# Row numbers of an indirect gather written by iota on GpSimd, and the gather moved to the head of GpSimd's list

## The chip, the cores and the metric

The kernel runs on one core of a Trainium2 chip. The metric is the device time of one execution in microseconds (us). A core has five engines that run their own instruction lists: TensorE (PE in the profile; PEld is its weight load), VectorE (DVE), ScalarE (ACT), GpSimd (POOL) and SyncE (SP). SP issues transfers only; POOL and ACT issue some as well. The transfers run on 16 DMA engines that all queues share: q1 in the profile carries what SP issues, q0 what POOL issues.

## The reference, cut to what matters

Two independent halves are computed and written side by side. The first is a linear attention with learned feature maps; the second, which this change touches, is a long convolution of `u` with a state-space kernel, done through a Fourier transform over 2L points.

```python
def _A_ref(x, wqkv, w_phi, wo):          # x: 1 x 2048 x 448, 16 heads of 28
    q, k, v = ...                        # x @ wqkv, split in heads
    phi_q = concat([softmax(q @ w_phi), softmax(-(q @ w_phi))])
    phi_k = concat([softmax(k @ w_phi), softmax(-(k @ w_phi))])
    o = (phi_q @ (phi_k^T @ v)) / (phi_q . sum_s phi_k + 1e-6)
    return o @ wo

def _B_ref(u, A_re, A_im, B_re, B_im, C_re, C_im, log_dt, Dskip):   # u: 1 x 2048 x 448, N = 256
    dt = exp(log_dt)
    P = exp(dt * (A_re + 1j A_im) * l)   # l = 0 .. 2047
    K = einsum("dn,dnl,dn->dl", C, P, dt * B).real
    y = irfft(rfft(pad(u)) * rfft(pad(K)))[:L]
    return y + u * Dskip

return concat([a, b], axis=-1)           # 1 x 2048 x 896
```

## The kernel before

The program is written as some 1,200 numbered units (an instruction or a few, with its tiles). A planner's result stands in the source as a written-out list, `ORDER`: each word is a unit's number and the engine that runs it (P, V, A, G, S for PE, DVE, ACT, POOL, SP). `Plan.run` records the units in that order, so each engine's list is the list of its own words, in their order. No scheduler moves them. Semaphore waits are put in where a unit reads or overwrites what another made. Transfers use eight semaphores per kind of queue in turn, so a transfer can also wait for the one eight places ahead of it.

The Fourier transform of `u` is done with the symmetry of the time axis: for each half `b` of 1,024 rows, `signal_spectrum` needs 512 rows in rising order and the 512 others mirrored. The first half of the tile `rw` comes by an ordinary load (unit 190 on SP, step `ua0.0`). The mirrored half comes by an indirect DMA (unit 191 on POOL, step `ua0.1`, line 610), which takes its 128 row numbers from the small tile `mirror` (128 x 2 int32, one column for each `b`). Each row is 3,584 bytes. `mirror` is filled by a load from a constant (unit 8 on POOL, step `rows`, line 446, issued in the helper `dma` at line 394).

Behind the gather, in the order in which they use each other:

- DVE, line 346: the difference and the sum of the two halves of `rw` (units 192 and 193, steps `ab0.0` and `ab0.1`).
- PE, line 379: the matmuls of the steps `us0.0` and `us0.1` (units 203, 196, 194, 201) with the cosine table `G1`, whose first half is loaded by unit 14 on SP. Their results are copied by ACT and DVE (line 369) and written to DRAM by transfers on SP and POOL (`SUd`).

Around it on POOL: unit 23 clears `zt`, which PE's idle matmuls at the start use (line 481); unit 17 clears the block-diagonal weight tile `BD` (line 464); units 19, 21 and 22 load pieces of `w_phi` into `BD`. The fourth piece, unit 20, stands in SP's list and waits for unit 17. Behind unit 20 in SP's list stand the loads of `G1` (14), of the attention weights (13), of `B_re` and `C_re` (5, 4), of a part of `x` (9), of the second half of `G1` (15), and then the first writes to `SUd`.

Of the kernel before, what the change touches and what calls it, by code (L numbers as in the profile page):

```python
# [50 lines left out]
def _round_bf16(a):  # L51
    import ml_dtypes
    return np.asarray(a, np.float32).astype(ml_dtypes.bfloat16)

def _row_positions():
    pos = np.full((N_KT, 128), -1)
    for kt, p0, h0, h1, runs in K_ROWS:
        r = p0
        for run in runs:
            for h in range(h0, h1):  # L60
                for lo in range(*run):
                    pos[kt, r] = HI[h] + LO[lo]
                    r += 1
    return pos

def _dft_tables():
    m = np.arange(512)
    w = np.pi * (4 * m + 1) / 2048.0
    phi = np.pi * np.outer(4 * m + 1, 4 * m + 1) / 4096.0
    GO = np.stack([np.cos(phi - np.pi / 4), np.cos(phi + np.pi / 4)])  # L70
    quad = np.arange(128)
    G = GO[:, np.stack([2 * quad, 2 * quad + 1, 510 - 2 * quad, 511 - 2 * quad])].transpose(2, 0, 1, 3)
    GO = GO.reshape(2, 4, 128, 512).transpose(2, 0, 1, 3)
    GI = np.stack([GO, GO[:, :, :, ::-1] * np.array([1.0, -1.0])[None, :, None, None]])
    e = _round_bf16(np.arange(2048)).astype(np.int64)
    pos = _row_positions()
    where = {int(p): (kt, r) for (kt, r), p in np.ndenumerate(pos)}
    assert set(e.tolist()) <= set(where)
    F = np.zeros((2, N_KT, 128, 4, 512))
    for blk in range(2):  # L80
        for l in range(1024):
            kt, r = where[int(e[1024 * blk + l])]
            even = np.exp(-1j * w * l) / 1024.0
            odd = np.exp(1j * (np.pi - w) * l) / 1024.0
            F[blk, kt, r] += np.stack([even.real, odd.real, even.imag, odd.imag])
    used = [(0, 0), (0, 1), (0, 2), (0, 3), (0, 4), (1, 4), (1, 5)]
    for blk in range(2):
        for kt in range(N_KT):
            assert (blk, kt) in used or not F[blk, kt].any()
    FT = np.stack([F[b, k] for b, k in used])  # L90
    FT = FT.reshape(7, 128, 16, 128).transpose(2, 1, 0, 3)
    pid = np.eye(128)[:, None, :] * np.array(DIAG).reshape(-1)[None, :, None]
    hm = np.zeros((112, 4, D_HEAD + 1))
    for hh in range(4):
        hm[hh::4, hh, :] = 1.0
    mirror = (256 * np.arange(2)[None, :] + 255 - np.arange(128)[:, None]).astype(np.int32)
    return (*(_round_bf16(t) for t in (G, GI, FT, pid, hm)), mirror)

ORDER = ("23G 42P 31P 43P 30P 33P 46P 0A 48A 49V 8G 32P 45P 38P 3S 1S 17G 2S 19G 6S 190S 50V 51V 53V 52V 56P 57V 54P 55A "
         "58P 59V 37P 84P 65A 63A 40P 64A 62A 85V 60P 82P 39P 61V 83V 191G 26P 25P 41P 47P 34P 27P 35P 44P 192V 193V 10S "  # L100
         "129P 20S 69A 70A 130V 66V 1098V 14S 125P 28P 29P 127P 126A 128V 13S 71V 203P 204A 196P 131P 194P 197A 201P 195V "
         "5S 132V 4S 202V 165P 153P 155P 166V 154V 156V 86P 78P 21G 88V 67A 72A 75A 73A 9S 89P 79A 80P 81A 15S 91V 167P "
         "151P 87V 90V 109A 108A 152V 117P 200S 198G 199G 118V 119P 168V 149P 120V 74V 22G 150A 207S 7S 12S 210P 211A 36P "
# [72 lines left out]
class Plan:  # L176
# [5 lines left out]
    def step(self, label, base, phase=None):  # L182

        self.now = label
        return phase
# [49 lines left out]
    def run(self):  # L235
        places, done = iter(PLACES), set()
        for word in ORDER.split():
            u, e = self.units[int(word[:-1])], ENGINES[word[-1]]
# [55 lines left out]
def kernel(  # L294
# [17 lines left out]
    nc = tc.nc  # L312
    out2 = out[0]
    x2 = A_x[0]
    u2 = B_u[0]
    consts = _dft_tables()
    G_d, GI_d, F_d, P_d, M_d, R_d = (nc.inline_tensor(t, name=f"const{i}").ap() for i, t in enumerate(consts))

    dram = ctx.enter_context(tc.tile_pool(name="dram", bufs=1, space=bass.MemoryType.DRAM))
    SUd = [dram.tile([128, 2, 2, 2, 4, CW * 2 * nq], BF16, name=f"SUd{i}") for i, nq in enumerate((2, 1, 1))]  # L320
# [3 lines left out]
    plan = Plan()  # L324
# [58 lines left out]
    def dma(engs, out_, in_, r=(), w=(), lat=None, cost=0.45, **kw):  # L383
        def run(ap):
            n = 1
            for st, m in ap.ap[:0:-1]:
                if st != n and m > 1:
                    break
                n *= m
            return 2 * n  # L390
        own = {"SP": cost, "POOL": max(cost, 0.7), "ACT": 0.65}
        piece = min(run(out_), run(in_), kw.get("max_dma_last_dim", 1 << 16))
        pieces = 2 * int(np.prod([n for _, n in out_.ap])) / piece
        plan.add({e: own[e] for e in engs}, lambda e=engs[0]: QUEUES[e].dma_start(out=out_, in_=in_, **kw), r, w, lat=lat,  # L394
                 load=pieces / 16000 * min(4 + 0.06 * piece, 28 + 0.0385 * piece) * (1.8 if kw else 1) + 0.02)
# [13 lines left out]
    mirror = sb("mirror", [128, 2], F32, oMISC + 576).bitcast(I32)  # L409
# [33 lines left out]
        step("in" + nm, 1)  # L443
        dma(["SP"], raw[nm][:, :, :], srcs[nm].rearrange("(j p) n -> p j n", j=4), w=[raw[nm][:, :, :]])
    step("rows", 1)
    dma(["SP", "POOL"], mirror[:, :], R_d, w=[mirror[:, :]])
    XS = [sb(f"xs{i}", [128, 4, D_MODEL], BF16, oW + 3584 * i) for i in range(4)]
    for i, t in enumerate(XS):
        step(f"inx{i}", 2)
# [148 lines left out]
    for v in V_:  # L598
# [7 lines left out]
        w=[DSK[:, :]])  # L606
# [328 lines left out]
    GI = [sb(f"GI{r}", [128, 2, 4, 512], BF16, oW + 8192 * r) for r in range(2)]  # L935
# [186 lines left out]
```

## Time and profile before

| | us |
|---|---|
| median of 3 runs (lowest to highest) | 303.56 (302.35 to 305.42) |
| the profiled execution's own time | 303.39 |
| its span, first to last instruction | 301.6 |

| engine | busy us | share of the span | instructions |
|---|---|---|---|
| PE | 265.5 | 88% | 4536 |
| DVE | 275.5 | 91% | 317 |
| ACT | 247.3 | 82% | 470 |
| POOL | 72.0 | 24% | 123 |

Busy shares are averages over stages with different limits. A timeline row has the start in us from the beginning of the span, the time of the row in us, engine, line, operation, tiles and count; in brackets stands how long the engine had been idle before it and what ended that. `SPq` rows are the issuing of transfers, not the transfers. A row of the chain of waits has start, length, and the work that the end hung on in that stretch.

### The profile page before, as it was taken

How to read it: one execution, taken by the hardware profiler on the slowest of the kernel's cores; microseconds unless marked ns; L12 is line 12 of the kernel's file. 1: busy time of each engine (PE TensorE's matmuls, PEld its weight loads, DVE VectorE, ACT ScalarE, POOL GpSimd, SP SyncE). 2: the span in 40 equal slices, each digit the busy share in tenths (PEclk: the TensorE clock that was granted, in tenths of full speed). 3: DMA queues.
4: the chain of work that ended last, by engine and by line, in shares of the span. 5: the costliest groups of instructions: out<-in, count | busy, mean ns of one | idle time of the engine just before them, and what ended most of it. 6: DMA issues, size and time to landing. Idle time of an engine off the chain costs nothing.

```text
span 301.6 us, 10486 instructions
## 1 busy us (share of the span) xinstructions
PE 265.5 (88%) x4536; PEld 216.4 (72%) x4536; DVE 275.5 (91%) x317; ACT 247.3 (82%) x470; POOL 72.0 (24%) x123
## 2 busy tenths in 40 slices
PE   7688999999989989989997779999778889979994
PEld 3345676786687677968865558788678787969994
DVE  2489999999999999999999999999988999999891
ACT  3859999999999999999799999999999734332431
POOL 5013131320211202000198000039900057600000
PEclk9979999999999999999999999999979999999998
DMA  6955841651120301021044300316976787776025
GB/s 192 301 165 153 243 116 30 186 93 33 30 65 18 78 2 48 4 48 47 8 56 85 91 19 9 103 24 165 245 274 171 236 270 190 183 211 212 17 73 172
DMA packets 40552, 35.20 MB, mean 117 GB/s; under 512 B 22110, under 2 KB 37719, under 8 KB 40379
## 3 DMA queue, kind: packets, MB, share of 16 engines
q1 hardware_dynamic: 34999, 30.53, 35.1%
q0 software_dynamic: 4320, 3.98, 6.8%
q8 instruction: 35, 0.57, 0.8%
q10 hardware_dynamic: 1188, 0.04, 0.2%
q14 instruction: 10, 0.08, 0.1%
HBM read 24.28 MB, written 7.34 MB: 105 GB/s over the span
## 4 chain that ended last, share of the span: by engine, by line
ACT 45%; DVE 18%; PE 16%; DMA 11%; issue 4%; SPq 3%; ACTq 1%; POOL 0%; DVEq 0%; POOLq 0%
ACT sbuf L359 33%; DVE sbuf L346 15%; ACT sbuf L369 8%; PE mm L379 7%; PE kb L379 5%; PE arg L379 4%; ACT L359 4%; DMA sbuf<-const 4%; DMA sbuf<-sbuf 3%; SPq L394 3%; DMA sbuf<-in_B_u_dram,sbuf 3%; DMA sbuf<-in_A_x_dram 2%; DVE sbuf L350 1%; DVE sbuf L369 1%; ACT sbuf L712 1%
## 5 line engine op out<-in xcount | busy, mean ns | idle before, releaser
L379 PEld LDWEIGHTS <-sbuf 128*32 128x32 bf16 (+4 forms) x4312 | 204.4, 118 | 72.2 <-issue 34.7
L346 DVE TENSOR_TENSOR sbuf<-sbuf 128x896 bf16<-128x896 bf16 (+6 forms) x197 | 216.9, 1137 | 10.4 <-ACT sbuf L359 4.6
L379 PE MATMUL mm<-sbuf 128*32 128x50 bf16 (+10 forms) x2257 | 145.1, 268 | 13.7 <-ACT sbuf L369 6.9
L359 ACT ACTIVATE sbuf<-arg 128x448 bf16<-128x448 f32 (+4 forms) x238 | 125.6, 645 | 0.7
L379 PE MATMUL kb<-sbuf 128*32 128x50 bf16 (+9 forms) x1153 | 74.2, 247 | 4.7 <-DMA sbuf<-sbuf 2.0
L394 POOL DMA_DIRECT2D sbuf<-sbuf x80 | 48.0, 634 | 113.7 <-ACT sbuf L369 95.4
L369 ACT CAST sbuf<-mm 128x448 bf16<-128x448 f32 (+4 forms) x96 | 54.2, 584 | 21.5 <-PE mm L379 18.0
L379 PE MATMUL arg<-sbuf 128*128 128x112 bf16 (+4 forms) x902 | 62.2, 219 | 8.5 <-ACT sbuf L359 5.5
L369 ACT CAST sbuf<-kb 128x448 bf16<-128x448 f32 (+3 forms) x42 | 23.0, 583 | 19.5 <-PE kb L379 16.1
L394 POOL DMA_DIRECT2D SUd<-sbuf x24 | 17.9, 749 | 62.6 <-ACT sbuf L369 42.6
L359 ACT ACTIVATE sbuf<-mm 112x512 bf16<-112x512 f32 x36 | 21.2, 648 | 0.3 <-PE mm L379 0.3
L346 DVE TENSOR_TENSOR sbuf<-arg,sbuf 128x896 bf16<-128x896 f32 (+1 forms) x21 | 20.4, 974 | 0.3 <-PE mm L379 0.2
L359 ACT ACT_TABLE_LOAD x14 | 18.0, 1283 | 1.4 <-PEq L1106 1.2
L359 ACT ACTIVATE sbuf<-sbuf 128x896 f32<-128x896 f32 (+2 forms) x12 | 11.7, 1017 | 1.9 <-DMA sbuf<-in_B_log_dt_dram 1.9
L712 ACT ACTIVATE sbuf<-sbuf 128x1680 bf16<-128x1680 bf16 x6 | 10.4, 1728 | 0.0
L574 PEld LDWEIGHTS <-sbuf 128*112 128x112 bf16 x64 | 5.3, 134 | 5.3 <-issue 4.9
L574 PE MATMUL kb<-sbuf 128*112 128x128 bf16 x64 | 6.0, 225 | 3.4 <-DVE sbuf L369 3.1
L785 PEld LDWEIGHTS <-sbuf 112*128 112x128 bf16 x128 | 7.3, 97 | 1.7 <-issue 1.0
L369 DVE CAST sbuf<-mm 128x448 bf16<-128x448 f32 (+1 forms) x11 | 6.6, 598 | 1.9 <-PE mm L379 1.7
L346 DVE TENSOR_TENSOR sbuf<-mm,sbuf 128x896 bf16<-128x896 bf16 (+1 forms) x13 | 7.4, 567 | 0.6 <-PE mm L785 0.5
L369 DVE COPY sbuf<-kb 112x512 bf16<-112x512 bf16 (+2 forms) x16 | 6.8, 436 | 0.5 <-PE kb L379 0.4
L363 ACT CAST sbuf<-sbuf 128x1792 bf16<-128x1792 f32 (+1 forms) x5 | 7.1, 1428 | 0.0
(37 smaller groups left out, 63.8 us busy)
## 6 DMA issues: line engine op xcount, KB each, us to landing
sbuf<-const SPq DMA_DIRECT2D x36, 224.0 KB
sbuf<-const SPq DMA_DIRECT2D x7, 512.0 KB
sbuf<-in_B_u_dram SPq DMA_DIRECT2D x6, 448.0 KB
sbuf<-in_A_x_dram SPq DMA_DIRECT2D x4, 448.0 KB
out_dram<-sbuf SPq DMA_DIRECT2D x16, 112.0 KB
sbuf<-SUd SPq DMA_DIRECT2D x1, 1792.0 KB
sbuf<-SUd SPq DMA_DIRECT2D x2, 896.0 KB
out_dram<-sbuf SPq DMA_DIRECT2D x8, 224.0 KB
```

What stands on the lines that cost most here:

```text
L346: lambda: nc.vector.tensor_tensor(out=at(out_), in0=at(a), in1=at(b), op=op), [whose(a), whose(b)], [out_])
L350: lambda: nc.vector.scalar_tensor_tensor(out=at(out_), in0=at(a), scalar=sc, in1=at(b), op0=op0, op1=op1),
L359: lambda: nc.scalar.activation(at(out_), at(a), func, scale=scale, bias=bias),
L363: plan.add({"ACT": 0.09 + count(out_) * 0.833e-3}, lambda: nc.scalar.copy(at(out_), at(a)), [whose(a)], [out_])
L369: lambda e: (nc.scalar.copy if e == "ACT" else nc.vector.tensor_copy)(at(out_), at(a)), [whose(a)], [out_])
L379: nc.tensor.matmul(out_, lhsT=lhsT, rhs=rhs, start=start, stop=stop, **kw)
L394: plan.add({e: own[e] for e in engs}, lambda e=engs[0]: QUEUES[e].dma_start(out=out_, in_=in_, **kw), r, w, lat=lat, load=pieces / 16000 * ...
L574: mms(p, [lambda t, j=j, x=x: nc.tensor.transpose(t[:, j, :], x[:, 112 * j:112 * j + 112], ident[:, :]) for j in range(4)], 0.4, [x, ident ...
L712: lambda en: nc.scalar.mul(m, m, -1.0) if en == "ACT" else nc.vector.tensor_scalar_mul(m, m, -1.0), [m], [m])
L785: mms(pt, [lambda t, i=i, s=s, c=c: nc.tensor.transpose(t[:, s, 112 * c:112 * c + 112], EKT[:, s, c, 128 * i:128 * i + 128], id112) for s ...
```

## The change

The constant with the row numbers is gone from the program, and unit 8 is no transfer any more: an iota on GpSimd writes the same 256 numbers into `mirror`. Unit 191, the first gather, moves up in `ORDER` from behind unit 83 to the place right behind unit 8. No other word of `ORDER` moves. On GpSimd's list the first instructions were

```
clear zt / load mirror / clear BD / load w_phi (19) / gather (191) / load w_phi (21) / ...
```

and are now

```
clear zt / library reload (L445) / iota mirror (L445) / gather (191) / clear BD / load w_phi (19) / load w_phi (21) / ...
```

The library reload isn't in the source. It is an instruction that the build puts ahead of the iota, on GpSimd, once in the program. In the built program SP's list is the same as before, including the wait of unit 20 for the clearing of `BD`. POOL issues one transfer fewer, so POOL's later transfers use the next semaphore of the eight.

```diff
-    mirror = (256 * np.arange(2)[None, :] + 255 - np.arange(128)[:, None]).astype(np.int32)
-    return (*(_round_bf16(t) for t in (G, GI, FT, pid, hm)), mirror)
+    return tuple(_round_bf16(t) for t in (G, GI, FT, pid, hm))
...
-ORDER = ("23G 42P 31P 43P 30P 33P 46P 0A 48A 49V 8G 32P 45P 38P 3S 1S 17G 2S 19G 6S 190S 50V ... 61V 83V 191G 26P ..."
+ORDER = ("23G 42P 31P 43P 30P 33P 46P 0A 48A 49V 8G 191G 32P 45P 38P 3S 1S 17G 2S 19G 6S 190S 50V ... 61V 83V 26P ..."
...
-    G_d, GI_d, F_d, P_d, M_d, R_d = (nc.inline_tensor(t, name=f"const{i}").ap() for i, t in enumerate(consts))
+    G_d, GI_d, F_d, P_d, M_d = (nc.inline_tensor(t, name=f"const{i}").ap() for i, t in enumerate(consts))
...
     step("rows", 1)
-    dma(["SP", "POOL"], mirror[:, :], R_d, w=[mirror[:, :]])
+    plan.add({"POOL": 0.2}, lambda: nc.gpsimd.iota(mirror[:, :], pattern=[[256, 2]], base=255, channel_multiplier=-1),
+             [], [mirror[:, :]])
```

## The prediction

> **What bounds the kernel now.** I read the chain of waits first, then the timelines of POOL, DVE, PE and SP in the first 20 us, then the rows on transfers. In order of time, the chain begins like this:
>
> ```profile
> 1.25 3.59 DMA sbuf<-const
> 5.12 8.11 DMA sbuf<-in_B_u_dram,sbuf
> 13.25 1.10 DVE sbuf L346
> 14.38 1.09 DVE sbuf L346
> 16.25 2.99 PE mm L379 x8
> ```
>
> The reader sees that the end hangs on the load of the row numbers, then on the gather, from 5.12 to 13.23. Behind it come the two DVE operations on its rows and the first matmuls of the signal's spectrum. So the piece that is edited lies on the path, at its head. What POOL does there:
>
> ```profile
> 0.74 0.12 POOL L481 MEMSET sbuf<- 128x32 bf16 x1 [0.29 <-POOLq L1106]
> 1.25 0.71 POOL L394 DMA_DIRECT2D sbuf<-const  x1 [0.39 <-issue]
> 1.96 0.50 POOL L464 MEMSET sbuf<- 112x448 bf16 x1
> 2.76 0.66 POOL L394 DMA_DIRECT2D sbuf<-in_A_w_phi_dram  x1 [0.30 <-POOL sbuf L464]
> 5.12 1.06 POOL L610 DMA_INDIRECT sbuf<-in_B_u_dram,sbuf  x1 [1.70 <-DMA sbuf<-const]
> ```
>
> Only 1.70 us of POOL's own time is spent waiting for the row numbers. The larger part is the gather itself: 8.11 us from its start to its landing. The second gather of the same size, at 50 us, takes 4.4 us from issue to landing, when the DMA engines have little else to do. In the first one's stage they are full: from 6 to 18 us the share in the table by stretches is 0.98 to 1.23. In the packets, the gather's data moves from 9.5 to 12 us. The users of the gather:
>
> ```profile
> 13.25 2.22 DVE L346 TENSOR_TENSOR sbuf<-sbuf 128x1792 bf16<-128x1792 bf16 x2 [3.08 <-DMA sbuf<-in_B_u_dram,sbuf]
> 12.13 0.60 PE L379 MATMUL mm<-sbuf 128*32 128x512 bf16 x2
> 15.86 0.39 PE L574 MATMUL kb<-sbuf 128*112 128x128 bf16 x4 [3.13 <-DVE sbuf L369]
> 16.08 3.16 PE L379 MATMUL mm<-sbuf 128*128 128x448 bf16 x8
> ```
>
> DVE is idle for 3.08 us, from 10.17 on, and PE for 3.13 us, since its next transposes need a buffer that DVE empties behind the two operations on the rows. After this the DVE and ACT timelines have few gaps until 40 us (DVE's largest is 1.28), and from 40 to 130 us ACT is busy 89.60 of 90 us. A delay or a gain at the head should therefore reach the end nearly whole; I pass it on one to one. Last, SP's list:
>
> ```profile
> 3.73 0.47 SPq L394 DMA_DIRECT2D sbuf<-in_A_w_phi_dram  x1
> 4.39 0.34 SPq L394 DMA_DIRECT2D sbuf<-const  x1
> 4.77 0.42 SPq L394 DMA_DIRECT2D sbuf<-in_A_wqkv_dram  x1
> ```
>
> The first of these is unit 20, which waits for POOL's clearing of `BD` (1.96 to 2.46); the second is the first half of `G1`, whose last landing in the trace is at 12.98. The matmuls at 16.08 need it too, so it stands only 3.1 us ahead of them.
>
> **The change part by part.** *Removed:* the load at 1.25 (0.71 us of POOL, 1 KB) and the wait of 1.70. *Added:* an iota of 128 x 2 numbers, which no row shows. The nearest is the 128 x 32 clearing at 0.12 us; from below 0.1 (the 128 x 1 clearings), from above 0.55 (the clearing of 128 x 448). I take 0.12. Then the gather waits for the iota's semaphore; the row of the same kind is the 0.30 between the `BD` clearing and the load that waits for it.
>
> *Added as well: the library reload ahead of the iota*, of L us, during which POOL does nothing else. No row shows one. From below it is 0: the library that serves the iota may be the one already there. It is an order to bring code from memory, so the nearest rows are POOL's own transfers in this stage: 3.6 us from issue to landing for the 1 KB load, 5.3 for the small pieces of `w_phi`, 8.11 for the 448 KB gather. One such trip is 3.6 to 8.1. Taking the old code out and the new in, or reading a table and then the code, is two trips in series: 10.6 at the small pieces' 5.3, and 16.2 at the gather's, which is the upper end. ACT's own reload of a table, 1.28 us, is a row of another engine with small tables, inside these bounds. I take 10.6, since a reload that fetches a whole library should not be cheaper than two of the small pieces.
>
> The Trainium skill (GPSIMD Engine Reference, section 2.1 Instruction dispatch) says that the first call to a freshly loaded GpSimd kernel pays about 6 us for loading its code, with no instruction in the profile that shows it. No trace here holds such a call. By that figure alone the estimate below would give a small gain, about 1.3 us, where mine gives a loss.
>
> *Moved:* the gather stands ahead of the `BD` clearing and of two `w_phi` loads. POOL then runs so: `zt` cleared at 0.86, reload, iota 0.12, gap 0.30, so the gather starts at 1.28 + L, its issue takes 1.06, the clearing of `BD` 0.50 and is done at 2.84 + L. This matters to SP: unit 20 goes at 3.14 + L (or 3.73, if that is later), and the load of `G1` 0.66 behind it, at 3.80 + L. Behind that stand, in order, the attention weights, `B_re`, `C_re`, `x` and the second half of `G1`.
>
> *The sum.* The gather starts when the loads ahead of unit 20 are nearly through (the last, of `x`, landed at 9.66) and SP adds nothing, so I give it the free 4.4 us: it lands at 5.7 + L, and the matmuls follow 2.83 us later as now (13.25 to 16.08), at 8.5 + L. `G1` is 512 KB: the free gather's 4.4, and about 0.6 for sharing the engines with the gather's end, so it lands at 8.8 + L. That is the later one. With L = 10.6 the matmuls start at 19.4 instead of 16.08, which is 3.3 us late. The loads behind `G1` come 10 us later at their issue, but in the trace they queued for the DMA engines: from the first data of `G1` at 7.5 to the last landing of its second half at 20.34 are 12.8 us, of which 1.6 are the gather's (448 KB at some 0.29 MB per us). Without the gather between them they need about 11.2, from 16.4 to 27.6. The first matmuls on it ran at 25.85 and would now run at 29.1, and the first part of `x` has as much room. So these loads add nothing, with 1.5 us to spare. The PE clock stays as it is there: granted at 0.53 from 16 to 18 us after the idle stretch, and the same after a longer one. The second gather and POOL's later transfers are not touched, since POOL idles 14.85 us behind these loads.
>
> The sum is made against the profiled execution, 303.39: 303.39 + 3.3 = **306.7**. The median of the runs is 0.2 above that execution, which I leave out.
>
> **The rivals.** *A, the reload costs nothing.* The library is there already and the order returns at once. Then the gather starts at 1.28 and, at the full stage's 8.11, lands at 9.4. The load of the other half landed at 8.54 and gets some 1.5 us later, since the gather's 448 KB now go ahead of it. DVE can start at 10.17, when it is free; the matmuls at 13.0, with `G1` at 12.98. That is 3.1 us early, and PE's idle stretch, which cost it the clock, is gone: 8 matmuls at 0.53 in 3.16 us would take some 1.7. DVE can use part of it, its gap of 1.28 at 20.46. Together 3.1 to 4.3; at 3.6 the time is 299.8. For it: nothing in the trace shows another library in use. Against it: the program does hold the instruction, by name a reload.
>
> *B, the reload is one trip.* With L = 5.3 the matmuls start at 14.1 and the time is 301.4; with 8.1, at 16.9 and 304.2. Break-even is at 7.3. For it: one trip is the simplest thing that a reload can be, and the skill's figure in the page named above falls here, at 6 us and some 302.1. Against it: that figure is for the first call after the load, and the load itself would come on top.
>
> *C, the shift is lost downstream.* The start moves by 3 us either way, but the stretch from 229 to 270 us, where the chain runs over transfers, takes it up; 303 to 304. For it: those loads could come early or late without the head. Against it: each is issued behind computed work, and the chain has no long stretch that hangs on nothing before it.
>
> **How the numbers follow.** Forecast, a reload of over 10.3 us: 0.45. A: 0.24. B: 0.23. C: 0.08. One per cent of the time is 3.0 us, about what a measurement of this kernel can tell from no change. Faster by over 1% is A, 0.24; within 1% are B and C, 0.31; slower by over 1% is the forecast, 0.45. The likeliest case's own range is 306.4 (L = 10.3) to 312.3 (L = 16.2, the matmuls at 25.0, 8.9 late). The range over all reaches to A at 299.5 and leaves out the last of the dear reloads: 299.5 to 311.0.
>
> **What would show it.** Right: POOL idle or in an unnamed instruction from 0.9 to about 11.5, the gather at 11.9, landing near 16.3, DVE's wait for it ending there; SP's `w_phi` load at 13.7 in place of 3.73; the DMA engines nearly idle between 10 and 13 us; the first 448-wide matmuls at 19.4. Wrong: the gather starting before 8 us, or landing before 13.2; the matmuls before 16; or the same shift at 20 us and none at 300.

## The result and the profile after

| | before | changed |
|---|---|---|
| median us (lowest to highest, 21 runs each) | 303.37 (300.28 to 306.12) | 300.17 (299.06 to 305.62) |
| profiled execution, us | 303.39 | 299.34 |
| span, us | 301.6 | 297.6 |

The ratio of the times is 0.9922, 95% interval 0.9897 to 0.9947: the changed kernel is 0.5 to 1.0% faster. The ratio, here and below, is that of the mean times without the runs that are more than 1.5% above the fastest of their kernel (four of before and one of changed), so it is not the quotient of the two medians. The forecast said 3.3 us slower. What happened is what the prediction called rival A.

The timeline of POOL in the changed kernel (start, length, engine, line, operation, tiles, count, and in brackets the idle time before it). The numbers of lines differ by a few from kernel to kernel, as lines were taken out or put in, and some rows are left out of the timelines:

```profile
0.74 0.12 POOL L481 MEMSET sbuf<- 128x32 bf16 x1 [0.29 <-POOLq L1106]
0.90 0.12 POOL L445 IOTA sbuf<- 128x2 int32 x1
1.71 1.21 POOL L610 DMA_INDIRECT sbuf<-in_B_u_dram,sbuf  x1 [0.68 <-POOL sbuf L445]
2.90 0.51 POOL L464 MEMSET sbuf<- 112x448 bf16 x1
3.72 1.30 POOL L393 DMA_DIRECT2D sbuf<-in_A_w_phi_dram  x2 [0.31 <-POOL sbuf L464]
```

The iota starts 0.04 us after the clearing of `zt` ends, and the gather at 1.71 instead of 5.12. The 0.04 us leave no room for a fetch. (The 0.68 us between the iota and the gather are 0.38 more than the 0.30 that the prediction took; no row tells why.) The rows of the iota's line show what became of that:

```profile
L445 POOLq MODIFY_POOL_CONFIG  x2: 11/11/11, 0.8 to 0.8; - x2
L445 POOL IOTA sbuf<- x1: 123/123/123, 0.9 to 0.9; 128x2 int32 x1
```

The columns are the shortest, median and longest duration in ns. The reload became two instructions of POOL's sequencer with 11 ns each, and the iota behind them didn't wait. The gather lands 5.8 us behind its start, at 7.51. The DVE timeline, where the wait of 3.08 us stood:

```profile
10.21 2.21 DVE L345 TENSOR_TENSOR sbuf<-sbuf 128x1792 bf16<-128x1792 bf16 x2
14.77 0.42 DVE L368 COPY sbuf<-kb 112x512 bf16<-112x512 bf16 x1 [0.91 <-PE kb L574]
17.27 0.62 DVE L368 CAST sbuf<-mm 128x448 bf16<-128x448 f32 x1
```

The wait is gone: DVE takes the rows when it is free, as it was in the kernel before at 10.17. Its first cast of the spectrum comes at 17.27 instead of 20.46, 3.19 us earlier. In the timeline of PE, a new wait has come up:

```profile
12.20 0.61 PE L378 MATMUL mm<-sbuf 128*32 128x512 bf16 x2
14.34 0.38 PE L574 MATMUL kb<-sbuf 128*112 128x128 bf16 x4 [1.54 <-ACT sbuf L368]
14.56 1.68 PE L378 MATMUL mm<-sbuf 128*128 128x448 bf16 x8
```

PE waits 1.54 us in place of 3.13, and no longer for DVE but for ACT. The matmuls are early by 1.52 us, not by 3.1; but the granted clock is 1.00 from 14 to 18 us where it was 0.53 from 16 to 18, and the eight take 1.68 us instead of 3.16. So they end 3.0 us earlier: half of the gain is the earlier start, and half the clock. (The clock of the kernel before is known from its one profiled execution.)

Pairing the instructions of the two traces one by one, PE and ACT run 2.99 us earlier at 26 us, 2.90 at 130 and 1.87 at 190. The last step goes with a dip of PE's granted clock in this execution (0.94 in its stretch from 157 to 188 us, where the kernel before has 1.00), and after it other dips and the transfers at the end put the difference at 4.05 at the end of the span. Of the 4.05, then, 2.9 are the change's, and the rest differs from run to run.

### The profile page after: what moved, and what is told of

It reads as the page before. It is cut to its first block, busy times and chain, and to the rows that moved or that the text cites. A ratio compares the mean times of both kernels' runs of the same rounds, so it can differ in the third digit from the quotient of the medians.

```text
span 297.6 us, 10488 instructions
## 1 busy us (share of the span) xinstructions
PE 263.8 (89%) x4536; PEld 215.4 (72%) x4536; DVE 275.7 (93%) x317; ACT 247.4 (83%) x470; POOL 71.5 (24%) x123
```

## The experiments

**The two parts of the change apart.** First the iota alone, with the gather at its old place in POOL's list:

```diff
-... 8G 191G 32P 45P ... 61V 83V 26P ...
+... 8G 32P 45P ... 61V 83V 191G 26P ...
```

> The iota alone; the gather keeps its old place in the list, behind the clearing of BD and one w_phi load. Theory (the gain is DVE's 3.08 us of waiting, which goes as soon as the gather lands before DVE is free at about 10.2 us): POOL runs reload, iota 0.9 to 1.0, BD clearing 0.5, w_phi 0.66, and the gather starts near 2.7 instead of 1.71; with the 5.8 to 6.5 us to landing it lands at 8.5 to 9.5, DVE does not wait, and the time is that of the changed kernel, 2.4 to 3.2 us below before. Rival (the gain is the gather's data moving ahead of the other loads, so that these land earlier): a gather one us later gives back part of it, 1 us or more.

The median is 300.24 us, ratio to before 0.9924 (0.9893 to 0.9956), the same as the changed kernel's. The gather starts at 2.89 and lands 7.7 us later, at 10.55 (I had expected 8.5 to 9.5), and DVE takes its rows directly behind its cast:

```profile
2.89 1.06 POOL L610 DMA_INDIRECT sbuf<-in_B_u_dram,sbuf  x1 [0.30 <-issue]
10.63 2.21 DVE L345 TENSOR_TENSOR sbuf<-sbuf 128x1792 bf16<-128x1792 bf16 x2
```

Moving the gather to the head added nothing to the iota, though there was no more than 0.1 us to spare.

Then the move alone, with the row numbers loaded as before:

```diff
-... 8G 32P 45P ... 83V 191G 26P ...
+... 8G 191G 32P 45P ... 83V 26P ...
```

> The gather at the head of POOL's list, but the row numbers loaded as before. Theory: POOL waits for the load until 4.85, the gather starts at about 5.1 as before, and the clearing of BD, now behind it, ends near 6.7 instead of 2.46, so SP's load of w_phi and the load of G1 behind it are issued some 2.9 us later (7.3 instead of 4.39). The DMA engines have fewer packets beside the gather, so it lands earlier than 13.23, near 11; G1 lands near 14. Together the matmuls start within 1 us of 16.08 and the time is within 1 us of before. Rival (the move brings the gain): 2 us or more below before.

The median is 299.80, ratio 0.9911 (0.9877 to 0.9944): this alone brings the gain as well. My expectation was wrong. The timeline of POOL in this kernel:

```profile
5.16 1.05 POOL L610 DMA_INDIRECT sbuf<-in_B_u_dram,sbuf  x1 [3.19 <-DMA sbuf<-const]
6.22 0.49 POOL L464 MEMSET sbuf<- 112x448 bf16 x1
```

and that of SP:

```profile
6.74 0.38 SPq L394 DMA_DIRECT2D sbuf<-in_A_w_phi_dram  x1
7.17 0.34 SPq L394 DMA_DIRECT2D sbuf<-const  x1
```

The gather starts when it always did, 5.16 against 5.12, but lands at 10.83 instead of 13.23. What changed is its company: the clearing of `BD` now holds SP's loads back, and `G1` is issued at 7.17 instead of 4.39. The packets of the gather show where the time went: the first moves at 7.79 instead of 9.61, and from there to the last they take as long as before (2.65 and 2.54 us). That SP's held loads are what let them begin earlier is the likely reason, since they are nearly all that stands elsewhere (one small load of `w_phi` on POOL went behind the gather too). `G1` lands at 13.24, hardly later than the 12.98 of before. DVE still waits, but 0.80 us, and the matmuls start at 13.71:

```profile
10.86 2.22 DVE L346 TENSOR_TENSOR sbuf<-sbuf 128x1792 bf16<-128x1792 bf16 x2 [0.80 <-DMA sbuf<-in_B_u_dram,sbuf]
13.71 1.68 PE L379 MATMUL mm<-sbuf 128*128 128x448 bf16 x8
```

I had the landings right (near 11 and near 14) and failed to add the 2.83 us from landing to matmuls to the first: that gives 13.8, not 16.

So the two parts don't add. Each takes away most or all of DVE's wait in its own way: an earlier issue, or a shorter trip. In the profiled executions the move alone is even the better one: from 30 to 130 us it runs 3.8 us ahead of before, the changed kernel 2.9. The wait for ACT that the changed kernel has is not in it, since in the built program all its tiles in PSUM stand where they did before. The times of the two don't tell them apart.

**The reload.** Eight of them in place of one:

```diff
+        for _ in range(8):
+            nc.gpsimd.load_library(library_config.standard)
         nc.gpsimd.iota(mirror[:, :], pattern=[[256, 2]], base=255, channel_multiplier=-1)
```

> The changed kernel with the library reload eight times in a row instead of once. Theory (the reload names the library that is already there and costs 22 ns of POOL's sequencer): 8 times 22 ns, so the iota starts about 0.15 us later than 0.90, and the time is that of the changed kernel. Rival (the fetch is hidden behind the first few us and each reload sends for the code): 7 more reloads delay the gather by over 5 us and the time rises above before.

The iota starts at 1.43 instead of 0.90, so a further reload costs 0.53 / 7 = 0.076 us. That is more than its rows (7 to 11 ns each, two to a reload), but a hundredth of the changes of library below. The median is 300.17, ratio 0.9919 (0.9886 to 0.9953). Then one operation ahead of the iota that lives in another library:

```diff
+        nc.gpsimd.memset(pad[:, 0:1], 0.0)
+        nc.gpsimd.partition_broadcast(pad[:, 1:2], pad[0:1, 0:1])
         nc.gpsimd.iota(mirror[:, :], pattern=[[256, 2]], base=255, channel_multiplier=-1)
```

> The changed kernel with a one-column partition broadcast on POOL ahead of the iota. It needs another library, so the build puts in a reload to that one and, ahead of the iota, a reload back. Theory (the reload is cheap only because its library is there already): two true changes of library, each some 6 us, so the iota comes at 8 to 15 us in place of 0.90, and by the law above the time is 2 to 8 us above before. Rival (a reload never costs more than its 22 ns): the iota at 1.5, the time as in the changed kernel.

The median is 312.07 against 302.21, ratio 1.0326 (1.0260 to 1.0392), 7.9 to 11.9 us slower, where I had expected 2 to 8. The timeline of POOL in this kernel:

```profile
0.80 0.10 POOL L448 MEMSET sbuf<- 128x1 f32 x1
8.58 0.28 POOL L449 PARTITION_BROADCAST sbuf<-sbuf  x1 [7.68 <-issue]
15.99 0.13 POOL L450 IOTA sbuf<- 128x2 int32 x1 [7.13 <-issue]
16.43 1.30 POOL L615 DMA_INDIRECT sbuf<-in_B_u_dram,sbuf  x1 [0.31 <-POOL sbuf L450]
```

Here the reloads are changes of library, and POOL stands still for 7.68 and 7.13 us behind them, with no row that fills the time: the rows of the reload itself are again 6 to 108 ns. The Trainium skill (GPSIMD Engine Reference, section 2.1 Instruction dispatch) says of the first call to a freshly loaded kernel that it pays about 6 us with no visible instruction. This trace agrees in kind and is 1.2 to 1.5 us longer: from the first row of the reload to the operation behind it are 7.49 and 7.21 us, against about 6. In the changed kernel the trace shows no such gap ahead of the iota, so the rule didn't apply.

**The rest of the prediction's sum.** If the reload's price was the only error, then a delay of that length put there by other means should cost what the prediction said. Four clearings of an unused tile ahead of the reload:

```diff
+    pad = sb("pad", [128, 1792], BF16, oT2)
...
+        for _ in range(4):
+            nc.gpsimd.memset(pad[:, :], 0.0)
         nc.gpsimd.iota(mirror[:, :], pattern=[[256, 2]], base=255, channel_multiplier=-1)
```

> The changed kernel with four clearings of an unused 128 x 1792 tile ahead of the reload on POOL, which stand for a reload that costs them in time. From the rows of 0.12 us for 32 columns and 0.50 for 448 one takes some 1.7 us, so L is about 7. The prediction's law (matmuls at 8.8 + L) says 15.8 and a time within 0.5 us of before. Rival (the gather's landing is set by the loads ahead of it in the DMA engines, not by its issue): it lands near 13, the matmuls start near 16, but the loads behind the w_phi load on SP, held until 10, land 3 us or more late and the time is 1 to 3 us above before.

The four take 6.54 us. The median is 302.66 against 302.21, ratio 1.0021 (0.9983 to 1.0059): no difference, which is what the sum says of a reload near break-even, but by luck. Two of its terms are off and cancel. The matmuls start 0.9 us later than before, not 0.8 us earlier, and they have the full clock, which the sum had not given them and which brings 1.5 us:

```profile
16.97 1.69 PE L378 MATMUL mm<-sbuf 128*128 128x448 bf16 x8 [0.47 <-DMA sbuf<-const]
```

With six:

> The changed kernel with six clearings of an unused 128 x 1792 tile ahead of the reload on POOL. Four of them took 6.5 us, so L is 9.8, near the 10.6 that the prediction gave the reload. With the terms as four clearings and the true library changes showed them (G1 lands 7.0 us behind its issue, not 5.0): gather at 11.1 and landing at 15.4, G1 issued at 13.3 and landing at 20.2, matmuls at 20.3, 4.2 us behind before, less the 1.5 us that the full clock brings where it is granted; the time 2.5 to 4.2 us above before. Rival (the loads behind are absorbed by slack): under 1.5 us above before.

The six take 9.84 us. The median is 307.57 against 303.02, ratio 1.0142 (1.0061 to 1.0223), 1.8 to 6.8 us slower. The waits of this kernel are the ones that the prediction named, DVE's for the gather:

```profile
15.34 2.22 DVE L345 TENSOR_TENSOR sbuf<-sbuf 128x1792 bf16<-128x1792 bf16 x2 [1.90 <-DMA sbuf<-in_B_u_dram,sbuf]
```

and PE's for `G1`, behind SP's held queue:

```profile
17.49 0.38 PE L579 MATMUL kb<-sbuf 128*112 128x128 bf16 x4 [1.01 <-ACT sbuf L368]
20.72 3.17 PE L378 MATMUL mm<-sbuf 128*128 128x448 bf16 x8 [2.85 <-DMA sbuf<-const]
```

The kernels set the landing of the gather and the start of the matmuls against the prediction's 5.7 + L and 8.8 + L (L here is the time from 0.86 to the iota):

| | L | gather lands, sum | measured | matmuls, sum | measured |
|---|---|---|---|---|---|
| four clearings | 6.5 | 12.2 | 11.95 | 15.3 | 16.97 |
| six clearings | 9.8 | 15.5 | 15.32 | 18.6 | 20.72 |
| two changes of library | 15.1 | 20.8 | 20.66 | 23.9 | 25.72 |

The gather's term holds within 0.3 us. The term of `G1` is too small by 1.7 to 2.1 us: it lands 7.0 us behind its issue with four clearings and with the changes of library, and 7.4 with six, where I took 5.0. So the reload's price was the step that turned the forecast, but not the only error of the sum: by these rows the loss at the price that I gave it would have been larger than I said.

**PE's new wait.** In the changed kernel the transposes at 14.34 write a buffer of the pair `kb`. In the kernel before they took the one that DVE empties (unit 130); in the changed one the build gives them the other one, which ACT empties (unit 126) behind its two sine operations, at 14.30. It is the only one of the 322 tiles in PSUM whose place differs between the two programs, and no word of the diff asks for it. Unit 126 given to DVE instead, right behind unit 130:

```diff
-... 130V 66V 1098V 14S 125P 28P 29P 127P 126A 128V ...
+... 130V 125P 126V 66V 1098V 14S 28P 29P 127P 128V ...
```

> The changed kernel, and unit 126, the copy of a transposed tile that PE waits for at 14.34, is done by DVE right behind unit 130 instead of by ACT behind its two sine operations. Theory (PE's 1.54 us wait in the changed kernel is for that copy): PE's next transposes start at 12.8 to 13.1 instead of 14.34, the 448-wide matmuls at 13.1 to 13.3 instead of 14.56, and DVE's first cast of their results at 16.0 to 16.2 instead of 17.27; the time falls by another 0.8 to 1.3 us. Rival (DVE's own list bounds this stretch): DVE takes on 0.35 us more work and the time stays or rises by up to 0.3 us.

The median is 299.77, ratio 0.9908 (0.9866 to 0.9949), no clear step from the changed kernel; and the profiled execution has PE's clock at 0.50 to 0.53 from 8 to 14 us, so that its early part says nothing. The kernel ran again beside the changed one:

> The same kernel as in the earlier run with unit 126 on DVE, whose profiled execution had PE's clock at 0.50 from 8 to 12 us, so that its start can't be read against the changed kernel's. In an execution with the full clock: theory (PE's wait of 1.54 us at 12.8 is for ACT's copy): transposes at 12.8 to 13.1, the 448-wide matmuls at 13.1 to 13.4, and everything from 24 to 150 us 0.8 to 1.3 us ahead of the changed kernel; the time 0.5 to 1.3 us below it. Rival: no more than 0.3 us ahead, since DVE has the copy's 0.35 us more to do.

> The changed kernel itself beside the others of this call: 2.0 to 3.2 us below before, as measured.

Now the profiled execution has the full clock. PE in it:

```profile
13.08 0.43 PE L574 MATMUL kb<-sbuf 128*112 128x128 bf16 x4
13.34 1.68 PE L378 MATMUL mm<-sbuf 128*128 128x448 bf16 x8
```

The wait is gone, the matmuls start at 13.34 (14.88 in the changed kernel's execution beside it), and from 30 to 130 us everything on PE is 4.1 us ahead of before, where the changed kernel is 2.7 ahead: 1.4 more. The median is 298.60, ratio 0.9843 (0.9785 to 0.9901), beside 299.81 and 0.9900 (0.9846 to 0.9953) for the changed kernel. The gain at the head is shown by the trace. That it stays in the time is not shown: the intervals overlap, and at the end of the span the two executions are 2.7 and 3.0 us ahead of before, this one behind one more dip of the clock. The edit also isn't as small as it looks, since 80 of the 322 tiles in PSUM change their place by it. The median of 298.60 is the lowest of all, but the same kernel had 299.77 the first time, no lower than the move alone.

## Why the prediction was wrong

- **The reload's price, L = 10.6.** This is the step that failed. The build's order names the library that is there already: 22 ns on the sequencer, and 0.04 us between the neighbours. That the library is what decides is shown by the two other kernels: seven more reloads of the same one cost 0.53 us, and a change to another one and back over 7 us each. I had the case as rival A and gave it 0.24, with "by name a reload" as the argument against it. The bounds from POOL's transfers were bounds on a fetch, and whether there was a fetch at all was the question. Even for a fetch 10.6 was too much: the two changes of library took 7.68 and 7.13 us, about as long as the 8.1 that rival B took for one trip at most, and with 7.2 the sum would have been near nought.
- **Rival A's own sum** gave 299.8; measured are 300.17. DVE free at 10.17: measured 10.21. Matmuls on the full clock, some 1.7 us: measured 1.68. The gain of 3.1 to 4.3: 2.9 to 3.0 until 130 us. The landing of the gather was placed at 9.4 and was 7.51, which made no difference, since DVE wasn't free. Its 13.0 for the matmuls was wrong: 14.56, by the new wait for ACT. That wait can't be seen in the diff, but stands in the built program, where the first of these transposes waits for ACT instead of DVE. So A came out near the measured time with the parts shifted: A had 3.1 us from the earlier start and 0.5 from the clock, and it was 1.5 from each.
- **The gather's trip.** The reading that the larger part of the path is the trip and not the wait for the row numbers was right, and went further than I took it: with the same issue time the trip is 8.11 us beside SP's loads and 5.7 with these held back.
- **SP's queue behind `BD`.** The mechanism is right (SP's `w_phi` load at 6.74, 9.53 and 18.25 when the clearing is late), and it is what costs the kernels with six clearings and with changes of library their time. `G1`'s term was mis-sized, 5.0 for 7.0 to 7.4. But a hold of 3 us, in the move alone, costs nothing, and seems to help the gather.
- **The PE clock.** That it would stay at 0.53 behind a longer idle stretch came out with six clearings (the eight matmuls take 3.17 us), and more than that with the changes of library, where 0.50 lasts until 31.3 us. With four clearings PE is idle only 0.47 us ahead of them, and the clock is full.
- **One to one to the end.** It held to 130 us in every kernel: a gain of 2.9 of 3.0 in the changed one, a loss of 4.7 of 4.6 with six clearings and of 10.4 of 10.6 with the changes of library. Behind that, single dips of PE's clock and the transfers at the end shift an execution by up to some 2 us either way.

## What to carry to other kernels

An instruction that the build puts in by itself must be priced by what it finds there: the reload cost under 0.1 us or over 7 us here, and the first question is which library is resident. A transfer on the path has a trip as well as an issue, and a change of what stands around it in the queues was worth as much here as an earlier start: one word moved in `ORDER` brought the whole gain without the iota. Once a wait is taken away, look for the next one at the same place, and compare the built programs' waits as well as the source, since a buffer can change hands without a word in the diff.

## What the runs showed of the hardware that I had not expected

Wide clearings on POOL slowed VectorE down in these kernels. Four scalings of 112 x 112 on DVE, which read and write bf16 in SBUF, took 0.72 us together in the changed kernel. With four clearings running on POOL beside them they took 1.84, and with the changes of library, where POOL stands still at that time, 0.73. With six clearings it was 3.29:

```profile
5.75 3.29 DVE L500 TENSOR_SCALAR sbuf<-sbuf 112x112 bf16<-112x112 bf16 x4
```

This delayed the first copies and ACT's sines in the kernels with clearings, but not what their matmuls waited for in the end. That the two engines get in each other's way at SBUF is stated in the Trainium skill (GPSIMD Engine Reference, section 8 Key points) for DVE instructions in some modes; the factor of over four is this trace's, and no run shows whether these scalings were in such a mode.

A change of library on GpSimd, to that of the partition broadcast and back, took 7.1 to 7.7 us and shows as idle time behind two rows of 6 to 108 ns, so a reader who adds up busy rows won't find it.
